# Pairing 64-row matmuls in the two halves of the TensorE array, with all eight PSUM banks in one rotation

## The chip, the cores and the metric

The kernel runs on one core of one Trainium2 chip. The metric is the device time of that core in microseconds (us), as the median of several executions. A profile comes from one of these executions; its span, from the first recorded instruction of the program to the end of the last, is about 1.7 us shorter than the timed value. For a kernel on one core, slow means over 1.5% above the fastest run of the same kernel. The medians are over all runs; where one of them was slow, the median of the fast ones stands beside it. Verdicts are given at 2%: "same" means that a difference of 2% isn't shown, not that there is none.

## The reference

Two branches over the same x are mixed with a gate. Branch A is a diagonal complex state-space scan over 2048 positions, branch B is a feed-forward network (FFN).

```python
x = A_x                                             # [1, 2048, 448]
g = sigmoid((x * gate_w).sum(-1, keepdims=True))
# A: Bu = x B_bar^T;  h_t = Lam_bar * h_(t-1) + Bu_t;  a = 2 Re(h C^T) + x * Dskip
# B: h = silu(x @ w1)          w1: [448, 1792]      "FFN1"
#    b = h @ w2                w2: [1792, 448]      "FFN2"
out = g * a + (1 - g) * b
```

FFN1 contracts over 448 rows. The array has 128 rows, so that is three full blocks and a remainder of 64 rows. This remainder is what the change is about.

## The kernel before

The program is written per engine. A small tracker gives every tile a name and makes an engine wait wherever it would read or overwrite a tile that another engine has not finished with. The eight PSUM banks are such tiles, `ps0` to `ps7`. Each engine runs its own list strictly in order.

FFN1 works in four chunks (even and odd positions, two halves each) of 14 blocks. The remainder is padded to 128 rows, with zeros in half of the rows of w1, so a block is four full matmuls:

```python
BK_F1 = [0, 1, 2, 3]                 # banks of FFN1
BK_F2 = BK_S = [4, 5, 6, 7]          # banks of FFN2, Bu, K0, Y
...
def ffn1(c, fb):
    bank = nxt(BK_F1, n_f1)
    ...
    def mm(pe):
        for j in range(4):           # 3 full blocks and one padded with 64 zero rows
            ins = pe.matmul(ps[:, bank, :], W[:, j, fb*128:(fb+1)*128],
                            XT[:, j0 + j, h*512:(h+1)*512], start=(j == 0), stop=(j == 3))
    T.op("pe", mm, reads=wk + xk, writes=[f"ps{bank}"])
    T.op("act", lambda e: e.activation(a[:, fb, :], ps[:, bank, :], AF.Silu), ...)
```

One small piece of branch A, the diagonal of Dskip, uses bank 7 by its number and not through a rotation:

```python
def side_diag():
    def mm(pe):                      # 4 matmuls with 2 rows (L464)
        ins = pe.matmul(ps[:, 7, pt*8:pt*8+2], RD[0:2, ...], ID[0:2, 0:2], ...)
    T.op("pe", mm, reads=["RD0", "RD1", "ID"], writes=["ps7"])
    T.op("dve", lambda e: e.tensor_copy(PV[:, :, 3:5], ps[:, 7, 0:32]...),   # L468
         reads=["ps7"], writes=["PVD"])
    ...                              # 8 small products, DE and DO
```

The order of the stages, which is each engine's order too:

```python
... ffn1(0, *) ; bu ; gate, scan(3) ; ffn1(1, *) ; scan(0) ; bu ; scan(1) ; scan(2)
ffn2(0, *) ; ffn1(2, *) ; ffn2(1, *)
run(coef)                            # side_diag, then CO and CE on VectorE
ffn1(3, *) ; ffn2(2, *) ; k0 ; ffn2(3, *) with ytile ...
```

VectorE comes to `side_diag`'s copy only when it has done all the scans.

Names in the profile lines: XT is x transposed; W1E and W1O hold w1 for even and odd positions, and until the gate is done the space of W1O holds a second copy of x (the line `W1O<-in_A_x_dram` is its load). Bu multiplies XT with LT, which holds the transposed B matrices; later the space of LT takes the results of FFN2. HS and Q belong to the scans on VectorE. CO and CE are tables that VectorE makes from C; K0 and Y are the last stages of branch A on TensorE, and K0 needs CO. A line such as `PE ps Lnnn <- DVE SG Lmmm: t, 1, t` says that TensorE's instruction at Lnnn waited for VectorE's at Lmmm, t us in all.

Of the kernel before, what the change touches and what calls it, by code (L numbers as in the profile page):

```python
# [8 lines left out]
AF = mybir.ActivationFunctionType  # L9

F32 = DT.float32
BF16 = DT.bfloat16
# [9 lines left out]
NFB = 14  # L22
NK = 1024
NKT = 8
# [120 lines left out]
def gated_mix(nc, A_x, A_Lambda_re, A_Lambda_im, A_B_re, A_B_im, A_C_re, A_C_im, A_log_dt,  # L145
              A_Dskip, B_x, B_w1, B_w2, gate_w, out):
    with ExitStack() as ctx:
        E = ctx.enter_context
        T = Tracker(nc, ctx)

        def sb(name, shape, dtype):
            return E(nc.sbuf_tensor(name, list(shape), dtype))
# [4 lines left out]
        XT = sb("XT", [128, 7, NK], BF16)  # L157
        W1E = sb("W1E", [128, 4, F_FF], BF16)
        W1O = sb("W1O", [128, 4, F_FF], BF16)
# [5 lines left out]
        CST = sb("CST", [112, 4, 256], BF16)  # L165
        CO = sb("CO", [128, 8, D], BF16)
        CE = sb("CE", [128, 8, D], BF16)
        KT = sb("KT", [128, 4, D], BF16)
        DE = sb("DE", [128, 4, 128], BF16)
        DO = sb("DO", [128, 4, 128], BF16)  # L170
# [3 lines left out]
        AT = [sb(f"AT{i}", [128, NFB, 512], BF16) for i in range(2)]  # L174
# [15 lines left out]
        Z = sb("Z", [128, 16], F32)  # L190
# [5 lines left out]
            return LTF[:, tile * D:(tile + 1) * D]  # L196

        ps = E(nc.psum_tensor("ps", [128, 8, 512], F32))
        BK_F1 = [0, 1, 2, 3]
        BK_F2 = BK_S = [4, 5, 6, 7]  # L200


        def ld(eng, dst, src, key, group=None):
            return T.dma(eng, lambda e: e.dma_start(dst, src), writes=[key], group=group)  # L204

        def ldt(dst, src, key, reads=(), group=None):
            return T.dma("sp", lambda e: e.dma_start_transpose(dst, src), reads=reads,
                         writes=[key], group=group)

        T.op("dve", lambda e: e.memset(Q1[:, 0, 0:512], 0.0), writes=["Q10"])  # L210
        T.op("dve", lambda e: e.memset(SG[0:64, 0:1], -1.0), writes=["SGa"])  # L211
# [10 lines left out]
        ld("act", W1E[0:64, 3, :], B_w1[384:448, :], "W1Ea")  # L222
        ld("act", W1E[:, 0:3, 0:512], B_w1[0:384, 0:512].rearrange("(j p) f -> p j f", p=128), "W1Eb")
        ld("act", W1E[:, 0:3, 512:], B_w1[0:384, 512:].rearrange("(j p) f -> p j f", p=128), "W1Ec")
        T.op("act", lambda e: e.activation(JK[:, 0, 0:1], HP[:, :], AF.Exp), reads=["HP"], writes=["JK0"])
        ldt(XT[:, 0:4, 0:512], x2[0:512, 0:512], "XTe0")
        ld("sp", BB[:, 0:6:2, D:], A_B_re[0:384, :].rearrange("(t p) d -> p t d", p=128), "Bre", gB)
        ld("sp", BB[:, 1:6:2, D:], A_B_im[0:384, :].rearrange("(t p) d -> p t d", p=128), "Bim", gB)
        ldt(XT[:, 4:7, 0:512], x2[0:512, 512:896], "XTo0")
        gB3 = T.group()  # L230
        for i, src in enumerate((A_B_re, A_B_im)):
            for h in range(2):
                ld("sp", Y3[h * 64:(h + 1) * 64, i, :], src[384:448, :], f"By{i}{h}", gB3)
        ldt(XT[:, 0:4, 512:1024], x2[512:1024, 0:512], "XTe1")
        ldt(XT[:, 4:7, 512:1024], x2[512:1024, 512:896], "XTo1")
        B_RAW = ["Bre", "Bim"]
        XC_ALL = ["XC0", "XC1"] + [f"XC3_{q}" for q in range(4)]
        B3 = ["By00", "By01", "By10", "By11"]
# [3 lines left out]
        T.op("pool", lambda e: e.affine_select(  # L242
            out=ID[:, :], in_=ID[:, :], pattern=[[-1, 128]], compare_op=ALU.is_equal, fill=0.0,
            base=0, channel_multiplier=1), reads=["ID"], writes=["ID"])
        T.op("pool", lambda e: e.memset(W1E[64:128, 3, :], 0.0), writes=["W1Ez"])
        T.op("pool", lambda e: e.iota(IOTA[:, :].bitcast(I32), pattern=[[1, NK]], base=0, channel_multiplier=0),
             writes=["IOTA"])
        T.op("pool", lambda e: e.tensor_copy(IOTA[:, :], IOTA[:, :].bitcast(I32)), reads=["IOTA"], writes=["IOTA"])
        T.op("pool", lambda e: e.memset(KT[64:128, 3, :], 0.0), writes=["KTz"])
        SGN = ["SGa", "SGb"]  # L250
# [3 lines left out]
             writes=["Rd"])  # L254
# [7 lines left out]
        def warm(n):  # L262
# [12 lines left out]
            reads=["ps6"], writes=["PV"])  # L275
# [12 lines left out]
        def c1(n, pt):  # L288
            i = pc(n)
            return P[:, i, pt:pt + 1]  # L290
# [32 lines left out]
        for o, up, low in (("ba", "lr", "li"), ("bb", "nli", "lr")):  # L323
# [10 lines left out]
            reads=["f2"] + SGN, writes=["f2s"])  # L334
# [47 lines left out]
        def step_B(pt):  # L382
            if pt < 3:
                lincombs([(BB[:, m, 0:D], f"BB{m}", BB[:, m, D:], c1("lr", pt), BB[:, m ^ 1, D:],
                           c1("li" if m % 2 else "nli", pt), B_RAW + ["lr", "li", "nli"])
                          for m in (2 * pt, 2 * pt + 1)])
# [62 lines left out]
        def side_C(odd):  # L449
            dst, key, b = (CO, "CO", "s") if odd else (CE, "CE", "e")  # L450
            for pt in range(3):
# [28 lines left out]
        XN = W1O[:, :, :].rearrange("p a b -> p (a b)")  # L480

        def load_xn():
            ld("sp", XN.rearrange("p (k c) -> p k c", k=NKT), x2.rearrange("(k p) c -> p k c", p=128), "XN")

        def gate():
            for t in range(2 * NKT):
                T.op("dve", lambda e, t=t: e.scalar_tensor_tensor(  # L487
                    JK[:, t % 2, :], XN[:, t * D:(t + 1) * D], 1.0, GWB[:, :],
                    ALU.mult, ALU.mult, accum_out=Z[:, t:t + 1]),
                    reads=["XN", "GW"], writes=[f"JK{t % 2}", f"Z{t}"])  # L490
                if t % 4 == 3:
                    yield
            yield
            zs = [f"Z{t}" for t in range(2 * NKT)]
            T.op("act", lambda e: e.activation(GT[:, 0, :], Z[:, :], AF.Tanh, scale=0.5),
                 reads=zs, writes=["GTt"])
            T.op("dve", lambda e: e.tensor_scalar(GT[:, 1, :], GT[:, 0, :], 0.5, 0.5, ALU.mult, ALU.add),
                 reads=["GTt"], writes=["GT1"])
            T.op("dve", lambda e: e.tensor_scalar(GT[:, 2, :], GT[:, 0, :], -0.5, 0.5, ALU.mult, ALU.add),
                 reads=["GTt"], writes=["GT2"])  # L500
            T.op("pool", lambda e: e.memset(W1O[0:64, 0, :], 0.0), writes=["XN", "W1Oz"])
            T.dma("sp", lambda e: e.dma_start(W1O[64:128, 0, :], B_w1[0:64, :]), reads=["W1Oz"],
                  writes=["W1Oa"])
            T.dma("sp", lambda e: e.dma_start(
                W1O[:, 1:4, :], B_w1[64:448, :].rearrange("(j p) f -> p j f", p=128)),
                reads=["W1Oz"], writes=["W1Ob"])
            yield


        n_f1 = [0]  # L510
        n_f2 = n_s = [0]

        def nxt(banks, n):
            b = banks[n[0] % len(banks)]
            n[0] += 1
            return b

        def ffn1(c, fb):
            odd, h = c // 2, c % 2
            bank = nxt(BK_F1, n_f1)  # L520
            W, j0 = (W1O, 3) if odd else (W1E, 0)
            a = AT[c % 2]
            wk = (["W1Oa", "W1Ob", "W1Oz"] if odd else
                  ["W1Ez", "W1Ea", "W1Eb"] if fb < 4 else ["W1Ez", "W1Ea", "W1Ec"])
            xk = [f"XTe{h}", f"XTo{h}"] if odd else [f"XTe{h}"]

            def mm(pe):
                ins = None
                for j in range(4):
                    ins = pe.matmul(ps[:, bank, :], W[:, j, fb * 128:(fb + 1) * 128],  # L530
                                    XT[:, j0 + j, h * 512:(h + 1) * 512],
                                    start=(j == 0), stop=(j == 3))
                return ins
            T.op("pe", mm, reads=wk + xk, writes=[f"ps{bank}"])
            T.op("act", lambda e: e.activation(a[:, fb, :], ps[:, bank, :], AF.Silu),  # L535
                 reads=[f"ps{bank}"], writes=[f"AT{c % 2}_{fb}"])

        def ffn2(c, q):
            odd, h = c // 2, c % 2
# [2 lines left out]
            a = AT[c % 2]  # L542
            bank = nxt(BK_F2, n_f2)

# [27 lines left out]
        def k0(j):  # L572
# [3 lines left out]
            def mm(pe):  # L576
                ins = None
                for m in range(7):
# [6 lines left out]
                 writes=[f"ps{bank}"])  # L585
            T.op("act", lambda e: e.activation(KT[0:M, j, :], ps[0:M, bank, 0:D], AF.Copy),
                 reads=[f"ps{bank}"], writes=[f"KT{j}"])

# [60 lines left out]
        def ytile(kt, odd):  # L649
            tile = 2 * kt + odd  # L650
            bank = nxt(BK_S, n_s)
            C, key = (CO, "CO") if odd else (CE, "CE")
            o0 = kt * 128 + (8 if odd else 7)
            t0 = kt * 128

            def mm(pe):
# [11 lines left out]
                else:  # L668
                    for j in range(4):
                        ins = pe.matmul(ps[:, bank, 0:D], XT[:, j, t0:t0 + 128], KT[:, j, :],  # L670
                                        start=False, stop=(j == 3))
                return ins
            xk = [f"XTe{kt // 4}", f"XTo{kt // 4}"]
            T.op("pe", mm, reads=hs_all + [f"{key}{m}" for m in range(7)] + xk
                 + [f"KT{j}" for j in range(4)] + ["KTz"] + [f"DO{j}" for j in range(4)],
                 writes=[f"ps{bank}"])
# [26 lines left out]
                    break  # L703

        tabs = chain(tables(0), tables(3))
        for fb in range(NFB):
            ffn1(0, fb)
            if fb in (8, 10, 12):
                run(tabs, 1)
        for h in range(2):  # L710
# [7 lines left out]
        s3 = scan(3)  # L718
        run(s3, 1)
        tabs = chain(tables(1), tables(2))  # L720
        for fb in range(NFB):
            ffn1(1, fb)
            if fb % 3 == 2:
                run(tabs, 1)
        run(gates)
# [16 lines left out]
        run(scan(2))  # L742
        for q in range(4):
            ffn2(0, q)
        for fb in range(NFB):
            ffn1(2, fb)
        for q in range(4):
            ffn2(1, q)
        run(coef)
        for fb in range(NFB):  # L750
            ffn1(3, fb)
        for q in range(4):
            ffn2(2, q)
        for j in range(4):
# [46 lines left out]
```

## Time and profile before

The median is 164.27 us over four runs (163.84 to 164.59); the first three gave 164.48 us.

| stage on TensorE, from the starts of its matmuls | starts at (us) | takes (us) |
|---|---|---|
| FFN1 chunk 0 (partly at half clock) | 10.20 | 14.68 |
| FFN1 chunk 1 | 33.95 | 12.09 |
| FFN1 chunk 2 | 68.72 | 12.09 |
| FFN2 chunk 1 | 80.80 | 10.69 |
| side diagonal | 91.49 | 0.18 |
| FFN1 chunk 3 | 91.67 | 12.10 |
| FFN2 chunks 2 and 3, K0, Y and the last store | 103.77 | 59.0 |

The next lines are from the first two parts of the page of the kernel before. The first line gives busy time by engine. The rows below it show 40 equal slices of the span (4.07 us each): busy tenths, and in the PEclk row the clock that TensorE was granted.

```profile
PE 154.5 (95%) x774; PEld 74.4 (46%) x774; DVE 109.8 (67%) x216; ACT 67.8 (42%) x111; POOL 7.3 (4%) x16
...
PE   6549999999999999999999999999999999999992
...
DVE  0559999306999999999999999999401131133342
...
PEclk9955999999999999999999999999999999999999
```

TensorE has hardly a gap after the start. VectorE's 67% hides a second, nearly full stretch: from slice 10 to slice 27 (the first is slice 0) it is 90% busy or more. So there is a second long chain close behind the first.

The chain of waits of the kernel before, in order of time (start, length, what), shows which of the two counts. These are pieces from its middle:

```profile
68.88 12.09 PE ps L530 x56
80.97 10.59 PE ps L548 x56
91.56 0.18 PE ps L464 x4
91.74 12.19 PE ps L530 x56
103.93 10.59 PE ps L548 x56
```

TensorE runs into itself, stage after stage. The head of the same view on the page, shares of the span by engine, says it in one line:

```profile
PE 92%; DMA 4%; ACTq 1%; DVE 0%; issue 0%
```

The waits of TensorE in the kernel before (for whom, us in total, times, longest) are all in the first 10.2 us:

```profile
PE ps L530 <- DMA W1E<-in_B_w_dram: 3.3, 1, 3.3
PE ps L266 <- DVE SG L211: 1.3, 1, 1.3
PE ps L259 <- issue: 0.6, 1, 0.6
```

Two lines of VectorE's timeline before (start, length, instruction, and in brackets the idle time ahead of it) give the ends of its stretch up to the diagonal's copy:

```profile
38.09 0.63 DVE L487 SCALAR_TENSOR_TENSOR JK<-W1O,GWB 128x448 bf16<-128x448 bf16 x1 [8.17 <-DMA W1O<-in_A_x_dram]
...
100.62 0.16 DVE L468 COPY PV<-ps 128x8 f32<-128x8 f32 x1
```

VectorE starts when x has landed a second time, at 38.07 us, and reads bank 7 at 100.62 us. TensorE wrote that bank at 91.5 us. The result lies in bank 7 for nine microseconds, and nobody else wants the bank: FFN1 has banks 0 to 3.

### The profile page before, as it was taken

Reading aid. Unit: us, or ns where it says so; the run is one execution under the profiler, and the core shown is the slowest. Engines: PE = TensorE matmul, PEld = TensorE weight load, DVE = VectorE, ACT = ScalarE, POOL = GpSimd, SP = SyncE. Lnnn points to the kernel's source line nnn. Section 1 sums busy time; section 2 is a strip of 40 time slices with the busy share of each in tenths; the row PEclk is TensorE's granted clock in tenths of the full one; section 3 lists DMA queues with packets and bytes.
Section 4 is the critical chain, followed back from the end, with each engine's and each line's share of the span. In section 5 each row is a group of like instructions: output and inputs, shape, how many; then the busy total and the mean of one; then the engine's idle time right before and its main releaser. Section 6 shows DMA issues by size and latency. Waiting matters only on the chain.

```text
span 162.8 us, 2017 instructions
## 1 busy us (share of the span) xinstructions
PE 154.5 (95%) x774; PEld 74.4 (46%) x774; DVE 109.8 (67%) x216; ACT 67.8 (42%) x111; POOL 7.3 (4%) x16
## 2 busy tenths in 40 slices
PE   6549999999999999999999999999999999999992
PEld 2113444444444455544455444455555555555551
DVE  0559999306999999999999999999401131133342
ACT  0614699759976522267622376431421101100000
POOL 7500000000030000000000000000000000000000
PEclk9955999999999999999999999999999999999999
DMA  4999999899207884000000000000000101101211
GB/s 101 265 354 214 211 174 141 165 365 352 69 0 229 260 154 89 14 0 0 4 0 0 0 0 0 6 0 0 0 0 0 60 0 56 56 0 71 101 57 56
DMA packets 26387, 14.76 MB, mean 91 GB/s; under 512 B 19845, under 2 KB 25226, under 8 KB 26378
## 3 DMA queue, kind: packets, MB, share of 16 engines
q1 hardware_dynamic: 25492, 13.03, 31.6%
q10 hardware_dynamic: 886, 1.61, 3.2%
q8 instruction: 6, 0.10, 0.3%
q14 instruction: 3, 0.02, 0.0%
HBM read 7.92 MB, written 1.84 MB: 60 GB/s over the span
## 4 chain that ended last, share of the span: by engine, by line
PE 92%; DMA 4%; ACTq 1%; DVE 0%; issue 0%
PE ps L530 31%; PE ps L548 26%; PE ps L659 13%; PE ps L564 13%; DMA W1E<-in_B_w_dram 4%; PE ps L670 4%; PE ps L579 3%; ACTq L204 1%; PE ps L666 1%; DVE OT L678 0%; PE ps L662 0%; PE ps L581 0%; PE ps L464 0%
## 5 line engine op out<-in xcount | busy, mean ns | idle before, releaser
L548 PE MATMUL ps<-W,AT 128*128 128x448 bf16 x224 | 43.5, 353 | 0.0
L535 ACT ACTIVATE AT<-ps 128x512 bf16<-128x512 f32 x56 | 32.7, 597 | 15.8 <-PE ps L530 15.7
L678 DVE SCALAR_TENSOR_TENSOR OT<-ps,GT,LT 128x448 bf16<-128x448 f32 x16 | 10.9, 684 | 33.6 <-PE ps L670 26.9
L548 PEld LDWEIGHTS ps<-W,AT 128*128 128x128 bf16 x224 | 21.7, 98 | 20.1 <-issue 0.2
L530 PE MATMUL ps<-XT,W1E 128*128 128x512 bf16 x112 | 27.1, 407 | 3.3 <-DMA W1E<-in_B_w_dram 3.3
L553 ACT ACTIVATE LT<-ps,GT 128x448 bf16<-128x448 f32 x16 | 10.1, 633 | 43.4 <-PE ps L548 43.4
L530 PE MATMUL ps<-XT,W1O 128*128 128x512 bf16 x112 | 24.5, 379 | 0.0
L564 PE MATMUL ps<-XT,LT 128*128 128x512 bf16 x98 | 21.5, 379 | 0.0
L530 PEld LDWEIGHTS ps<-XT,W1E 128*128 128x128 bf16 x112 | 11.5, 103 | 18.8 <-issue 7.3
L530 PEld LDWEIGHTS ps<-XT,W1O 128*128 128x128 bf16 x112 | 10.9, 98 | 12.9
L600 DVE TENSOR_TENSOR_SCAN G<-P,Q 128x1024 f32<-128x1024 f32 x7 | 15.7, 2277 | 0.0
L564 PEld LDWEIGHTS ps<-XT,LT 128*128 128x128 bf16 x98 | 9.6, 98 | 11.6
L487 DVE SCALAR_TENSOR_TENSOR JK<-W1O,GWB 128x448 bf16<-128x448 bf16 x16 | 8.8, 622 | 8.2 <-DMA W1O<-in_A_x_dram 8.2
L659 PE MATMUL ps<-CO,HS 128*128 128x448 bf16 x56 | 11.9, 352 | 0.0
L659 PE MATMUL ps<-CE,HS 128*128 128x448 bf16 x56 | 11.9, 352 | 0.0
L568 ACT ACTIVATE HS<-ps 128x512 bf16<-128x512 f32 x14 | 8.4, 598 | 6.8 <-PE ps L564 6.6
L597 DVE TENSOR_TENSOR Q<-G,SIN 128x1024 bf16<-128x1024 f32 x7 | 8.5, 1218 | 0.0
L597 DVE TENSOR_TENSOR Q<-G,COS 128x1024 bf16<-128x1024 f32 x7 | 8.5, 1209 | 0.0
L659 PEld LDWEIGHTS ps<-CO,HS 128*128 128x128 bf16 x56 | 5.5, 98 | 5.1
L670 PE MATMUL ps<-KT,XT 128*128 128x448 bf16 x32 | 7.4, 352 | 0.0
L659 PEld LDWEIGHTS ps<-CE,HS 128*128 128x128 bf16 x56 | 5.3, 98 | 4.4
L266 PE MATMUL ps<-Q 128*128 128x512 bf16 x12 | 4.8, 569 | 1.3 <-DVE SG L211 1.3
(75 smaller groups left out, 114.9 us busy)
## 6 DMA issues: line engine op xcount, KB each, us to landing
W1O<-in_A_x_dram SPq DMA_DIRECT2D x1, 1792.0 KB, 9.8
out_dram<-OT SPq DMA_DIRECT2D x8, 224.0 KB, 1.9
W<-in_B_w_dram SPq DMA_DIRECT2D x1, 1568.0 KB, 14.0
W1O<-in_B_w_dram SPq DMA_DIRECT2D x1, 1344.0 KB, 7.4
W1E<-in_B_w_dram ACTq DMA_DIRECT2D x1, 960.0 KB, 9.7
W1E<-in_B_w_dram ACTq DMA_DIRECT2D x1, 384.0 KB, 7.3
BB<-in_A_B_re_dram SPq DMA_DIRECT2D x1, 336.0 KB, 6.8
BB<-in_A_B_im_dram SPq DMA_DIRECT2D x1, 336.0 KB, 8.6
```

The source lines that it names most:

```text
L487: T.op("dve", lambda e, t=t: e.scalar_tensor_tensor(JK[:, t % 2, :], XN[:, t * D:(t + 1) * D], 1.0, GWB[:, :], ALU.mult, ALU.mult, accum_o ...
L530: ins = pe.matmul(ps[:, bank, :], W[:, j, fb * 128:(fb + 1) * 128], XT[:, j0 + j, h * 512:(h + 1) * 512], start=(j == 0), stop=(j == 3))
L535: T.op("act", lambda e: e.activation(a[:, fb, :], ps[:, bank, :], AF.Silu), reads=[f"ps{bank}"], writes=[f"AT{c % 2}_{fb}"])
L548: ins = pe.matmul(ps[:, bank, 0:D], a[:, fb, q * 128:(q + 1) * 128], W2[:, fb, :], start=(fb == 0), stop=(fb == NFB - 1))
L553: T.op("act", lambda e: e.activation(bs(tile), ps[:, bank, 0:D], AF.Copy, scale=GT[:, 2, tile:tile + 1]), reads=[f"ps{bank}", "GT2"], writ ...
L564: ins = pe.matmul(ps[:, bank, :], LT[:, m, j, :], XT[:, j, h * 512:(h + 1) * 512], start=(j == 0), stop=(j == 6))
L568: T.op("act", lambda e: e.activation(HS[:, m, 8 + h * 512:8 + (h + 1) * 512], ps[:, bank, :], AF.Copy), reads=[f"ps{bank}", f"F{pt}"], wri ...
L597: T.op("dve", lambda e: e.tensor_tensor(o, a, b, op), reads=reads, writes=writes)
L600: T.op("dve", lambda e: e.tensor_tensor_scan(G[:, c, :], rb, Q1[:, c, :], 0.0, ALU.mult, ALU.add), reads=[f"Q1{c}", "rr"], writes=[f"G{c}"])
L659: ins = pe.matmul(ps[:, bank, 0:D], HS[:, m, o0:o0 + 128], C[:, m, :], start=(m == 0), stop=False)
L670: ins = pe.matmul(ps[:, bank, 0:D], XT[:, j, t0:t0 + 128], KT[:, j, :], start=False, stop=(j == 3))
L678: T.op("dve", lambda e: e.scalar_tensor_tensor(o[:, odd * D:(odd + 1) * D], ps[:, bank, 0:D], GT[:, 1, tile:tile + 1], bs(tile), ALU.mult, ...
```

## The change

The intent is to stop spending a full matmul on 64 rows. The two remainders of a pair of blocks are run at the same time, one in the lower and one in the upper 64 rows of the array. For that, the 64 rows of w1 are loaded into both halves, and a copy `XR` of the matching rows of x is made with its halves swapped (four copies from SBUF to SBUF). Four blocks form a batch: 12 full matmuls, then two pairs. A batch holds four banks at once, so all stages now share one rotation of eight.

```diff
-        BK_F1 = [0, 1, 2, 3]
-        BK_F2 = BK_S = [4, 5, 6, 7]
+        BK_F1 = BK_F2 = BK_S = list(range(8))
...
+        def xr_early(h):                       # on the sync queue
+            T.dma("sp", lambda e: e.dma_start(XR[64:128, hs], XT[0:64, 3, hs]), reads=[f"XTe{h}"], ...)
+            T.dma("sp", lambda e: e.dma_start(XR[0:64, hs], XT[64:128, 3, hs]), reads=[f"XTe{h}"], ...)
...
+        ld("act", W1E[64:128, 3, :], B_w1[384:448, :], "W1Ez")   # was a memset to zero
...
         ldt(XT[:, 4:7, 0:512], ..., "XTo0")
+        xr_early(0)
         ... Y loads; ldt XTe1; ldt XTo1
+        xr_early(1)
...
-        n_f1 = [0]
-        n_f2 = n_s = [0]
+        n_f1 = n_f2 = n_s = [0]
...
+            for fb, bank in zip(fbs, banks):
+                def mm(pe, ...):               # three full matmuls of each block
...
+            def rest(pe):
+                for i, (fb, bank) in enumerate(zip(fbs, banks)):
+                    up = (i % 2 == 1 and not single) != bool(odd)
+                    p = slice(64, 128) if up else slice(0, 64)
+                    x = XT[p, 3, hs] if up == bool(odd) else XR[p, hs]
+                    ins = pe.matmul(ps[:, bank, :], W[p, jr, ...], x, start=False, stop=True)
...
+            for f0 in range(0, NFB, 4):
+                yield from ffn1(c, list(range(f0, min(f0 + 4, NFB))), single and f0 == 0)
```

`side_diag` is not touched. (The very first batch is unpaired, `single`, so that it need not wait for the copies. The loads of W1O lose a memset that they used to wait for.)

More of the change, by code (lines that the diff above doesn't have):

```diff
@@ L167, in gated_mix @@
         CE = sb("CE", [128, 8, D], BF16)
+        XR = sb("XR", [128, NK], BF16)
         KT = sb("KT", [128, 4, D], BF16)
@@ L208, in ldt @@
                          writes=[key], group=group)
+        def xr_early(h):
+            hs = slice(h * 512, (h + 1) * 512)
+            T.dma("sp", lambda e: e.dma_start(XR[64:128, hs], XT[0:64, 3, hs]), reads=[f"XTe{h}"],
+                  writes=[f"XR{h}a"])
+            T.dma("sp", lambda e: e.dma_start(XR[0:64, hs], XT[64:128, 3, hs]), reads=[f"XTe{h}"],
+                  writes=[f"XR{h}b"])
         T.op("dve", lambda e: e.memset(Q1[:, 0, 0:512], 0.0), writes=["Q10"])
@@ L244, in gated_mix @@
             base=0, channel_multiplier=1), reads=["ID"], writes=["ID"])
-        T.op("pool", lambda e: e.memset(W1E[64:128, 3, :], 0.0), writes=["W1Ez"])
         T.op("pool", lambda e: e.iota(IOTA[:, :].bitcast(I32), pattern=[[1, NK]], base=0, channel_multiplier=0),
@@ L483, in load_xn @@
             ld("sp", XN.rearrange("p (k c) -> p k c", k=NKT), x2.rearrange("(k p) c -> p k c", p=128), "XN")
+        XN_DONE = [f"Z{2 * NKT - 1}"]
         def gate():
@@ L500, in gate @@
                  reads=["GTt"], writes=["GT2"])
-            T.op("pool", lambda e: e.memset(W1O[0:64, 0, :], 0.0), writes=["XN", "W1Oz"])
-            T.dma("sp", lambda e: e.dma_start(W1O[64:128, 0, :], B_w1[0:64, :]), reads=["W1Oz"],
+            T.dma("sp", lambda e: e.dma_start(W1O[0:64, 0, :], B_w1[0:64, :]), reads=XN_DONE,
+                  writes=["W1Oz"])
+            T.dma("sp", lambda e: e.dma_start(W1O[64:128, 0, :], B_w1[0:64, :]), reads=XN_DONE,
                   writes=["W1Oa"])
@@ L505, in gate @@
                 W1O[:, 1:4, :], B_w1[64:448, :].rearrange("(j p) f -> p j f", p=128)),
-                reads=["W1Oz"], writes=["W1Ob"])
+                reads=XN_DONE, writes=["W1Ob"])
             yield
-        n_f1 = [0]
-        n_f2 = n_s = [0]
+        n_f1 = n_f2 = n_s = [0]
         def nxt(banks, n):
@@ L516, in nxt, with ffn1 @@
             return b
-        def ffn1(c, fb):
+        def ffn1(c, fbs, single=False):
             odd, h = c // 2, c % 2
-            bank = nxt(BK_F1, n_f1)
-            W, j0 = (W1O, 3) if odd else (W1E, 0)
+            hs = slice(h * 512, (h + 1) * 512)
+            W, w0, x0, jr = (W1O, 1, 4, 0) if odd else (W1E, 0, 0, 3)
             a = AT[c % 2]
             wk = (["W1Oa", "W1Ob", "W1Oz"] if odd else
-                  ["W1Ez", "W1Ea", "W1Eb"] if fb < 4 else ["W1Ez", "W1Ea", "W1Ec"])
+                  ["W1Ez", "W1Ea", "W1Eb"] if fbs[-1] < 4 else ["W1Ez", "W1Ea", "W1Ec"])
@@ L525, in ffn1 @@
             xk = [f"XTe{h}", f"XTo{h}"] if odd else [f"XTe{h}"]
-            def mm(pe):
-                ins = None
-                for j in range(4):
-                    ins = pe.matmul(ps[:, bank, :], W[:, j, fb * 128:(fb + 1) * 128],
-                                    XT[:, j0 + j, h * 512:(h + 1) * 512],
-                                    start=(j == 0), stop=(j == 3))
-                return ins
-            T.op("pe", mm, reads=wk + xk, writes=[f"ps{bank}"])
-            T.op("act", lambda e: e.activation(a[:, fb, :], ps[:, bank, :], AF.Silu),
-                 reads=[f"ps{bank}"], writes=[f"AT{c % 2}_{fb}"])
+            banks = [nxt(BK_F1, n_f1) for _ in fbs]
@@ new lines, in ffn1, with mm @@
+            for fb, bank in zip(fbs, banks):
+                def mm(pe, fb=fb, bank=bank):
+                    ins = None
+                    for j in range(3):
+                        ins = pe.matmul(ps[:, bank, :], W[:, w0 + j, fb * 128:(fb + 1) * 128],
+                                        XT[:, x0 + j, hs], start=(j == 0), stop=False)
+                    return ins
+                T.op("pe", mm, reads=[k for k in wk if k != "W1Ez"] + xk, writes=[f"ps{bank}"])
+            def rest(pe):
+                ins = None
+                for i, (fb, bank) in enumerate(zip(fbs, banks)):
+                    up = (i % 2 == 1 and not single) != bool(odd)
+                    p = slice(64, 128) if up else slice(0, 64)
+                    x = XT[p, 3, hs] if up == bool(odd) else XR[p, hs]
+                    ins = pe.matmul(ps[:, bank, :], W[p, jr, fb * 128:(fb + 1) * 128], x,
+                                    start=False, stop=True)
+                return ins
@@ new lines, in ffn1, with ffn1_chunk @@
+            T.op("pe", rest, reads=[k for k in wk if k != "W1Ez" or not single] + xk + ([] if single else [f"XR{h}a", f"XR{h}b"]),
+                 writes=[f"ps{bank}" for bank in banks])
+            for fb, bank in zip(fbs, banks):
+                T.op("act", lambda e, fb=fb, bank=bank: e.activation(a[:, fb, :], ps[:, bank, :], AF.Silu),
+                     reads=[f"ps{bank}"], writes=[f"AT{c % 2}_{fb}"])
+                yield
+        def ffn1_chunk(c, single=False):
+            for f0 in range(0, NFB, 4):
+                yield from ffn1(c, list(range(f0, min(f0 + 4, NFB))), single and f0 == 0)
@@ L705, in gated_mix @@
         tabs = chain(tables(0), tables(3))
-        for fb in range(NFB):
-            ffn1(0, fb)
+        for fb, _ in enumerate(ffn1_chunk(0, single=True)):
             if fb in (8, 10, 12):
@@ L720, in gated_mix @@
         tabs = chain(tables(1), tables(2))
-        for fb in range(NFB):
-            ffn1(1, fb)
+        for fb, _ in enumerate(ffn1_chunk(1)):
             if fb % 3 == 2:
@@ L744, in gated_mix @@
             ffn2(0, q)
-        for fb in range(NFB):
-            ffn1(2, fb)
+        for fb, _ in enumerate(ffn1_chunk(2)):
+            pass
         for q in range(4):
@@ L749, in gated_mix @@
         run(coef)
-        for fb in range(NFB):
-            ffn1(3, fb)
+        for fb, _ in enumerate(ffn1_chunk(3)):
+            pass
         for q in range(4):
```

## The prediction

> **What bounds it now.** The chain of waits gives TensorE 92% of the 162.8 us span: from 10.2 us to 159.7 us the matmuls run back to back. In the timeline, full 512-column matmuls start 0.216 us apart. FFN1 is 224 of them (four chunks of 14 blocks x 4), 12.09 us a chunk when warm.
> Close behind runs VectorE: it starts the gate products when the second copy of x lands (38.07 us) and is then busy almost without a gap until 115.9 us. The copy of the diagonal out of PSUM bank 7 (L468) starts at 100.62 us, 8.9 us after TensorE wrote it (L464, 91.6 us). Nobody minds before, because FFN1 uses banks 0-3 only.
>
> **Intended gain.** 26 pairs of 64-row matmuls in place of 52 full ones: 26 x 0.216 = 5.6 us if the pairs overlap. The Trainium skill, "TensorEngine Tiling (Array Packing)", Key Properties, says that changing the tiling mode drains TensorE. The trace agrees: around the two-row matmuls of L464 about 0.10 us going in and 0.07 us coming out are lost. 16 batches x 0.17 = 2.7 us back, so about 2.9 us net on TensorE.
>
> **What it costs.**
> 1. The side diagonal still writes bank 7, and FFN1 now rotates through all eight. Chunk 3's eighth block falls on bank 7; the built program shows a VectorE wait there. So TensorE stops after 16 + 9 matmuls of chunk 3 until VectorE has finished the last scan and L468. Earlier gains only lengthen this stop.
> 2. VectorE gets later. The sync queue now waits for the transposes of x (XT of the second half landed at 18.40 us) and issues four copies (about 0.6 us each, as the Y loads took) before the seven LT transposes, which started at 17.16 us. I expect them some 3.8 us later and the load of x (issued 28.23 us, 9.8 us to landing) about 2.5 us later. VectorE then reaches L468 at about 103.1 us.
> 3. TensorE reaches block 7 of chunk 3 at about 96 us and idles some 7 us. "TensorE: Matmul & The Clock Gate", Part 1, gives a window of about 3.4 us after which an idle array falls to half clock. This trace agrees: its clock was 0.5 from 8.7 to 15.5 us after the early gap. I expect half clock again for 3.4 to 6.8 us, about 2.5 us lost.
>
> **Sum.** Stop ends at 103.4 us. Left of chunk 3: 21 full matmuls + 5 pairs = 26 x 0.216 = 5.6 us, six mode changes 0.5 us, cold clock 2.5 us: FFN1 ends at about 112 us, against 103.93 us. From there TensorE bounds as before. +8.1 us: **172.5 us**, range 169.8 to 175.0. Chances: faster by over 2% 0.03, within 2% 0.05, slower by over 2% 0.92.
>
> **What would show it.** A TensorE wait of 5 to 9 us in chunk 3, released by VectorE's L468; a second half-clock stretch in the clock row just after; L468 at 101 to 105 us; the x load landing 1 to 4 us later; chunk 2 of FFN1 shorter than 12.09 us by about 0.8 us, pairs starting a few ns apart; everything from the third FFN2 chunk on unchanged in length.
>
> **What would make it wrong.** If the x load is not delayed, 170 us. If the pairs don't overlap, only about 1 us more shows. If the wait on bank 7 were not there: about 162 us.

## The result, and the profile after

The changed kernel takes 173.24 us (172.80 to 173.35, four runs) against 164.27 us. The ratio is 1.0543, with a 95% interval of 1.0509 to 1.0576. Here and below, a ratio is the mean time of one kernel's fast runs over that of the other's fast runs of the same rounds, so it is not quite the ratio of the medians quoted. The output is correct.

| stage on TensorE | before: starts, takes | after: starts, takes |
|---|---|---|
| FFN1 chunk 0 | 10.20, 14.68 | 9.77, 13.83 |
| FFN1 chunk 1 | 33.95, 12.09 | 32.68, 11.42 |
| FFN1 chunk 2 | 68.72, 12.09 | 66.78, 11.41 |
| FFN2 chunk 1 | 80.80, 10.69 | 78.20, 11.58 |
| side diagonal | 91.49, 0.18 | 89.78, 0.17 |
| FFN1 chunk 3 | 91.67, 12.10 | 89.95, 22.54 |
| everything later | 103.77, 59.0 | 112.49, 59.0 |

The whole loss is in one line. TensorE comes to chunk 3 of FFN1 1.7 us earlier than before and leaves it 8.7 us later; the rest is equal. The sum over chunk 3: 8.26 us of stop and about 2.7 us of half clock (both shown below), less the 0.7 us that the pairs save, make about the 10.4 us by which it is longer. The corresponding lines of the page of the changed kernel (40 slices of 4.29 us) show the place:

```profile
PE 154.9 (90%) x774; PEld 69.8 (41%) x774; DVE 108.8 (63%) x216; ACT 63.5 (37%) x111; POOL 4.1 (2%) x14
...
PE   7679999999999999999989208999999999999992
...
DVE  0567999103999999999999999996000311323332
...
PEclk9969999999999999999999955799999999999999
```

TensorE is nearly idle in slices 22 and 23 (94 to 103 us), and its clock drops in slices 23 to 25. VectorE is full in both of these slices. The chain of waits of the changed kernel, by engine, now runs through VectorE for 43% of the span, where it had none of it before:

```profile
DVE 43%; PE 38%; DMA 8%; SPq 8%; issue 1%
```

The waits of TensorE in the changed kernel name what ended the idle time:

```profile
PE ps L543 <- DVE PV L477: 8.3, 1, 8.3
...
PE ps L473 <- ACT LT L583: 0.8, 1, 0.8
```

L477 is the copy out of bank 7, L468 of before. The second line is a smaller thing of the same kind: FFN2's rotation ended on bank 7 just before the diagonal (L473), which therefore waits 0.8 us for ScalarE to empty it. The timeline of both engines around the stop:

```profile
93.18 2.12 PE L543 MATMUL ps<-XT,W1O 128*128 128x512 bf16 x9
...
103.34 0.16 DVE L477 COPY PV<-ps 128x8 f32<-128x8 f32 x1
...
103.55 1.46 PE L543 MATMUL ps<-XT,W1O 128*128 128x512 bf16 x3 [8.26 <-DVE PV L477]
...
105.92 4.38 PE L543 MATMUL ps<-XT,W1O 128*128 128x512 bf16 x12
...
110.76 1.47 PE L543 MATMUL ps<-XT,W1O 128*128 128x512 bf16 x6
```

Nine matmuls are blocks 4, 5 and 6 of chunk 3; the next three, of block 7, go to bank 7 and wait 8.26 us. The 12 full matmuls at 105.92 us take 4.38 us where 12 full ones elsewhere take 2.76 us. The clock records of the trace put half clock from 99.0 to 109.2 us.

The pairs themselves do what they were made for. These lines are from chunk 2, with the matmul form as rows*columns of the array:

```profile
69.47 0.39 PE L554 MATMUL ps<-XT,W1O 64*128 64x512 bf16 x1
69.47 0.39 PE L554 MATMUL ps<-XR,W1O 64*128 64x512 bf16 x1
69.69 0.38 PE L554 MATMUL ps<-XT,W1O 64*128 64x512 bf16 x1
69.70 0.38 PE L554 MATMUL ps<-XR,W1O 64*128 64x512 bf16 x1
70.01 2.76 PE L543 MATMUL ps<-XT,W1O 128*128 128x512 bf16 x12
```

The two of a pair start together (3 ns apart in the raw records), and the next pair follows after 0.22 us. Between the last pair and the full matmuls lie 0.31 us, 0.09 us more than the usual spacing of 0.216 us: this is the mode change.

The sync queue's timeline explains why VectorE is later. It begins the gate products when the x load has landed; in the changed kernel this is:

```profile
41.52 0.63 DVE L498 SCALAR_TENSOR_TENSOR JK<-W1O,GWB 128x448 bf16<-128x448 bf16 x1 [10.80 <-DMA W1O<-in_A_x_dram]
```

The sync queue, first before, then after:

```profile
12.66 4.39 SPq L207 DMA_TRANSPOSE XT<-in_A_x_dram  x2
17.16 10.39 SPq L207 DMA_TRANSPOSE LT<-BB  x7
...
28.23 0.43 SPq L204 DMA_DIRECT2D W1O<-in_A_x_dram  x1
```

```profile
14.15 3.80 SPq L207 DMA_TRANSPOSE XT<-in_A_x_dram  x2
19.31 0.48 SPq L212 DMA_DIRECT2D XR<-XT  x1
19.83 0.60 SPq L214 DMA_DIRECT2D XR<-XT  x1
20.55 9.77 SPq L207 DMA_TRANSPOSE LT<-BB  x7
...
30.99 0.43 SPq L204 DMA_DIRECT2D W1O<-in_A_x_dram  x1
```

The queue waits 1.3 us for x's transposes before it can issue the last two copies, and everything behind them moves: the LT transposes by 3.4 us, the x load by 2.8 us. The x load lands 3.4 us later (41.49 us), and VectorE copies bank 7 2.7 us later.

### The profile page after: what moved, and what is told of

It reads as the page before. It is cut to its first block, busy times and chain, and to the rows that moved or that the text cites. A ratio compares the mean times of both kernels' runs of the same rounds, so it can differ in the third digit from the quotient of the medians.

```text
span 171.5 us, 2024 instructions
## 1 busy us (share of the span) xinstructions
PE 154.9 (90%) x774; PEld 69.8 (41%) x774; DVE 108.8 (63%) x216; ACT 63.5 (37%) x111; POOL 4.1 (2%) x14
## 4 chain that ended last, share of the span: by engine, by line
DVE 43%; PE 38%; DMA 8%; SPq 8%; issue 1%
DVE Q L627 17%; PE ps L578 12%; PE ps L689 12%; DVE G L630 9%; DMA W1O<-in_A_x_dram 6%; SPq L207 5%; DVE JK L498 5%; PE ps L543 4%; PE ps L700 4%; PE ps L609 3%; DVE HS L627 3%; SPq L204 2%; DMA Y<-in_A_B_im_dram 2%; DVE BB L387 2%; DVE HS L357 1%; DVE G L355 1%
## 5 line engine op out<-in xcount | busy, mean ns | idle before, releaser
L560 ACT ACTIVATE AT<-ps 128x512 bf16<-128x512 f32 x56 | 29.5, 605 | 34.3 <-PE ps L554 34.3
L543 PE MATMUL ps<-XT,W1O 128*128 128x512 bf16 x84 | 21.9, 412 | 8.3 <-DVE PV L477 8.3
L583 ACT ACTIVATE LT<-ps,GT 128x448 bf16<-128x448 f32 x16 | 10.1, 633 | 42.1 <-PE ps L578 40.1
L543 PE MATMUL ps<-XT,W1E 128*128 128x512 bf16 x84 | 21.2, 404 | 2.9 <-issue 2.9
L543 PEld LDWEIGHTS ps<-XT,W1O 128*128 128x128 bf16 x84 | 8.0, 103 | 21.1 <-DVE PV L477 8.8
L543 PEld LDWEIGHTS ps<-XT,W1E 128*128 128x128 bf16 x84 | 8.1, 103 | 15.9 <-issue 7.7
L598 ACT ACTIVATE HS<-ps 128x512 bf16<-128x512 f32 x14 | 7.9, 615 | 0.3 <-POOL HS L370 0.3
L275 PE MATMUL ps<-Q 128*128 128x512 bf16 x12 | 5.5, 627 | 1.3 <-DVE SG L218 1.3
## 6 DMA issues: line engine op xcount, KB each, us to landing
W1E<-in_B_w_dram ACTq DMA_DIRECT2D x1, 960.0 KB, 10.1
```

The lines of the kernel that those rows point to most:

```text
L543: ins = pe.matmul(ps[:, bank, :], W[:, w0 + j, fb * 128:(fb + 1) * 128], XT[:, x0 + j, hs], start=(j == 0), stop=False)
L560: T.op("act", lambda e, fb=fb, bank=bank: e.activation(a[:, fb, :], ps[:, bank, :], AF.Silu), reads=[f"ps{bank}"], writes=[f"AT{c % 2}_{fb}"])
L583: T.op("act", lambda e: e.activation(bs(tile), ps[:, bank, 0:D], AF.Copy, scale=GT[:, 2, tile:tile + 1]), reads=[f"ps{bank}", "GT2"], writ ...
```

## The experiments

The theory has three parts. (A) The eight-bank rotation makes FFN1 need bank 7, which the diagonal holds until VectorE is through with its scans. (B) The copies in the sync queue make VectorE later and the stop longer. (C) The stop lets the clock fall, which costs more. The main rivals are that the pairing with its mode changes costs more than it saves, and that the extra DMA traffic, rather than its place in the queue, is the delay. All runs below gave correct output. Each has one profile. How far one profile can be trusted shows in two of the same program: the copy of bank 7 began at 103.34 us in the changed kernel and at 104.18 us when the same kernel was run again. Runs of one group ran on the same chip, beside the same runs of the kernel before.

### First group: the parts alone (before: 163.45 us)

**rot8_alone.** The kernel before with the rotation and nothing else:

```diff
-        BK_F1 = [0, 1, 2, 3]
-        BK_F2 = BK_S = [4, 5, 6, 7]
+        BK_F1 = BK_F2 = BK_S = list(range(8))
...
-        n_f1 = [0]
-        n_f2 = n_s = [0]
+        n_f1 = n_f2 = n_s = [0]
```

> The kernel before with nothing but the single rotation of eight banks. If the stop on bank 7 is the cause, FFN1 chunk 3 must stop here too: TensorE should reach its eighth block at about 98.5 us (91.7, plus 0.7 us for an eviction of bank 7 ahead of the side diagonal, plus seven blocks of 0.864) and wait for VectorE's copy of the diagonal until 100.8 us: about 3 us in all, 167.3 us, no new half-clock stretch [...]. If the rotation is harmless and the pairing or the copies are the cause, 164.3 us.

Measured: 168.47 us (168.24 us without the one slow run of four), ratio 1.0258 (1.0171 to 1.0345; with three fast runs the interval is wide and the verdict at 2% is unclear). Of TensorE's waits in this run, two belong to bank 7:

```profile
PE ps L528 <- DVE PV L467: 3.4, 1, 3.4
...
PE ps L463 <- ACT LT L551: 0.8, 1, 0.8
```

Both waits are there without a pair, a copy or a mode change. Chunk 3 takes about 15.66 us against 12.10 (its first matmul is missing from the records; from the diagonal's first matmul to the next FFN2 chunk it is 15.84 us against 12.28). This settles (A). The stop is 1.1 us longer than expected, since in this run TensorE got there earlier and VectorE later than I had put down; there is no second half-clock stretch in the profiled run (the slow run, 171.70 us, has no profile). The stop is shorter than in the changed kernel because TensorE comes later and VectorE earlier. A faster TensorE only waits longer here.

**seven_banks.** The changed kernel, with bank 7 left to the diagonal:

```diff
-        BK_F1 = BK_F2 = BK_S = list(range(8))
+        BK_F1 = BK_F2 = BK_S = list(range(7))
```

> The changed kernel with bank 7 left out of the rotation (seven banks). If the stop on bank 7 is the whole loss: no long TensorE wait in chunk 3, no half-clock stretch, and the net gain of the pairing (about 2.4 us by the batch periods of the changed kernel's trace) shows: 162 us, between 161 and 163. If the pairing with its mode changes or the later VectorE chain are themselves the loss, it stays above 164.3 us.

Measured: 162.13 us, ratio 0.9898 (0.9846 to 0.9950). One line of code takes back the loss and leaves a gain of 1%, small but clear of the noise. The stop is gone, and there is no half clock in the middle. What is left of the lateness shows in two new, small waits of TensorE in this kernel:

```profile
PE ps L594 <- DMA LT<-BB: 0.6, 1, 0.6
PE ps L609 <- issue: 0.4, 1, 0.4
```

The first is the first Bu stage waiting for a late LT transpose. The second stands ahead of the K0 stage (L609), which needs CO: VectorE finished CO at 112.3 us, and K0 began at 112.4 us, with the FFN2 chunk ahead of it 0.58 us longer than elsewhere. The view says "issue" for it; that it is CO I infer from these times. So the second chain is right behind the first again.

**seven_unpaired.** The same with all remainders in the same half, so that none can overlap; batches, copies and mode changes stay:

```diff
-                    up = (i % 2 == 1 and not single) != bool(odd)
+                    up = bool(odd)
```

> As seven_banks, but all 64-row matmuls go to the same half of the array, so none can overlap; batches, mode changes and copies stay. If the pairs overlap fully, this is 26 x 0.216 = 5.6 us slower than seven_banks: about 167.6 us. If the pairing gains nothing, the same as seven_banks.

Measured: 167.40 us, ratio 1.0204 (1.0133 to 1.0275; unclear at 2%), 5.3 us above seven_banks. The four remainders of a batch now follow each other, four in 1.03 us:

```profile
73.06 1.03 PE L554 MATMUL ps<-XT,W1O 64*128 64x512 bf16 x4
```

A clean figure comes from the traces, away from the start where the clock wavers. From the first matmul of FFN2 chunk 0 to that of FFN2 chunk 1, which spans one whole FFN1 chunk, it is 22.68 us before, 22.01 us in the changed kernel and 23.51 us here. The pairs save 1.50 us a chunk, seven times 0.216 us, so they overlap fully. Against the kernel before, the eight mode changes of a chunk cost 0.83 us, or 0.10 us each. The rival that pairing is a loss falls; it is a net gain of 0.67 us a chunk, though more than half of the gross gain goes to the mode changes.

**copies_on_act.** The changed kernel, with the four copies issued by ScalarE's queue:

```diff
-            T.dma("sp", lambda e: e.dma_start(XR[64:128, hs], XT[0:64, 3, hs]), ...)   # and the other
+            T.dma("act", lambda e: e.dma_start(XR[64:128, hs], XT[0:64, 3, hs]), ...)
...
         pact("cs", col("afr"), AF.Sin, ...)
+        xr_early(0)
...
         for fb, _ in enumerate(ffn1_chunk(0, single=True)):
+            if fb == 6:
+                xr_early(1)
```

> The changed kernel with the four copies issued by ScalarE's queue, which has nothing to do at those moments, in place of the sync queue. If the sync queue's wait and issue time make VectorE late, the x load lands at 38 to 39 us again, L477 starts at about 101 us, and the time falls by about 2.2 us to 171 us. If it is the extra DMA traffic that makes it late, it stays at 173.2 us.

Measured: 171.11 us, ratio 1.0447 (1.0381 to 1.0512): the expected time, but not by the expected way. The x load landed at 39.4 us, 2.1 us earlier than in the changed kernel and still 1.3 us later than before, so the place in the queue is most of the delay. The remaining 1.3 us are there already when the LT transposes are issued (18.41 us against 17.16 before), since the queue spent longer on the transposes of x ahead of them. Whether the extra DMA traffic does that was not tested. But L476, the copy of bank 7, began at 102.52 us, only 0.8 us earlier. The remaining 1.2 us of the gain came from the clock: half clock from 99.1 to 105.9 us, so that chunk 3 took 7.7 us after the stop and not 8.9 us. Part of this may be chance: the changed kernel run again (after_again, below) took 8.3 us there. One line of VectorE's timeline in this run shows where the rest of the earlier x load went:

```profile
59.27 0.69 DVE L626 TENSOR_TENSOR HS<-Q 128x1024 bf16<-128x1024 bf16 x1 [1.19 <-DMA Q<-Q]
```

### Second group: what was left open (before: 163.98 us)

**swap_first.** VectorE waited there for the two half swaps `Q<-Q` of a scan. The W1O loads stand ahead of these swaps in the same queue, as they did before; the change makes them three in place of two and lets them start 0.03 us after VectorE's last gate product in place of 1.7 us. Here the loads go behind the swaps:

```diff
-            T.dma("sp", ... W1O ...)      # three loads, at the end of gate()
+            yield
+        def load_w1o(): ...               # the same three loads
...
         run(s3, 1)
+        load_w1o()
```

> The kernel copies_on_act with the three W1O loads issued after the two half swaps of the third scan in place of before them. In copies_on_act the x load landed 2.1 us earlier than in the changed kernel but L476 started only 0.8 us earlier, and VectorE waited 1.2 us for the swap's landing. If the swap was held up behind the W1O loads, the wait goes and L476 starts at about 101.3 us: about 1.2 us less than copies_on_act, 169.9 us. If not, L476 stays at 102.5 us and the time at 171.1 us.

Measured: 170.91 us, ratio 1.0429 (1.0382 to 1.0477). The wait is gone (the second swap landed 2.3 us after its issue, in place of 4.8 us), and L476 began at 101.54 us, 1.0 us earlier, as expected. This is one profile each; the same wait was 0 us in the changed kernel and 0.75 us in after_again, so the size is uncertain. The time did not follow: chunk 3 took 8.4 us after the stop against 7.7 us in copies_on_act, since half clock lasted until 106.3 us. What the earlier end of the stop gives, the moment at which the clock recovers takes back in part. This is a miss in time and a hit in mechanism.

**stop_filled.** The changed kernel, with 34 useless matmuls into bank 0 (which is empty by then) ahead of the stopped block. The stop stays; only TensorE is busy in it:

```diff
             for fb, bank in zip(fbs, banks):
+                if c == 3 and fb == 7:
+                    def fill(pe):
+                        for _ in range(34):
+                            ins = pe.matmul(ps[:, 0, :], W[:, 1, 0:128], XT[:, 4, hs], start=True, stop=True)
+                    T.op("pe", fill, ..., writes=["ps0"])
```

> The changed kernel with 34 useless matmuls (7.3 us warm) put into bank 0 just ahead of the stopped block, so that TensorE works while it would idle; the wait on bank 7 and its end at 103.5 us stay. If the half clock after the stop is a loss of its own, chunk 3 ends at about 109.8 us in place of 112.5, the clock row has no second dip, and the time is about 170.4 us. If the clock after the stop costs nothing, 173.2 us.

Measured: 171.83 us (171.38 us without the one slow run of four), ratio 1.0470 (1.0407 to 1.0533), less of a gain than expected. In the profiled run the clock stayed full and chunk 3 took 6.25 us after the stop against 8.94 us, but L477 began at 105.06 us, 1.7 us later than in the changed kernel. The filling cannot have caused that: VectorE's scan that began at 64.55 us in the changed kernel began at 66.27 us here, 1.7 us late already, some thirty microseconds before the first useless matmul. The pair was run again on one chip all the same (third group).

**diag_early.** A repair that keeps eight banks: the copies on ScalarE's queue as in copies_on_act, and the whole diagonal moved to where VectorE idles for the x load:

```diff
+        ld("act", RD[0:1, 0:D], row(A_Dskip), "RD0", gRD)      # and RD1, behind the W1E loads
...
-        coef = chain(side_coef(), side_diag(), side_C(True), side_C(False))
+        coef = chain(side_coef(), side_C(True), side_C(False))
...
         load_w2()
+        run(side_diag())
         run(gates, 5)
```

> The repaired change: copies on ScalarE's queue, and the side diagonal (its two loads, four matmuls, copy and eight products) moved to about 34 us, where VectorE idles for the x load; eight banks and batches of four stay. No stop on bank 7, and VectorE about 1.6 us ahead of copies_on_act, so CO is ready before TensorE asks. TensorE bound throughout: 0.68 us saved in each of three chunks and some 0.4 us in the first: about 2.4 us under before.

Measured: 162.02 us, ratio 0.9901 (0.9858 to 0.9944). The copy of bank 7 runs at 33.4 us, CO is finished at 108.9 us, and K0 starts without a wait at 111.4 us. TensorE bounds again, and the gain is about 2 us in medians (1.6 us by the ratio), a little less than the expected 2.4 us.

**six_six_two.** The same with larger batches:

```diff
-            for f0 in range(0, NFB, 4):
-                yield from ffn1(c, list(range(f0, min(f0 + 4, NFB))), single and f0 == 0)
+            for f0, f1 in ((0, 4), (4, 10), (10, 14)) if c == 0 else ((0, 6), (6, 12), (12, 14)):
+                yield from ffn1(c, list(range(f0, f1)), single and f0 == 0)
```

> As diag_early with batches of 6, 6 and 2 blocks (4, 6, 4 in the first chunk), so six mode changes in a chunk in place of eight. At the 0.10 us a change that the unpaired run gives (0.83 us a chunk over eight), about 0.2 us less in each chunk: 0.8 us under diag_early, unless ScalarE, which now gets six blocks at once, makes TensorE wait for banks.

Measured: 161.67 us, ratio 0.9874 (0.9836 to 0.9911). From FFN2 chunk 0 to FFN2 chunk 1 it is 21.80 us against 22.00 us in diag_early: the 0.2 us a chunk are there. In total only 0.35 us show, because TensorE waited 1.0 us for an LT transpose at the first Bu stage. The intervals of the two kernels overlap.

### Third group: the clock again, and a better kernel (before: 164.04 us)

**after_again** is the changed kernel unaltered, and **stop_filled_again** is stop_filled unaltered, on one chip.

> The changed kernel unaltered, to stand beside stop_filled on one chip, since the runs so far were on different chips or at different times: 173 us, the stop ending at 103 to 104 us, half clock after it.

> stop_filled unaltered. In its first run chunk 3 took 6.25 us after the stop against 8.94 us in the changed kernel, but its stop ended 1.7 us later, so the time fell by less than expected. If the half clock costs 2.7 us of its own, then on the same chip this is 2 to 3 us under after_again, with the stop ending at the same time in both. If the filling itself delays VectorE, the stop ends later again and the difference is about 1 us.

Measured: 173.58 us (173.43 us without the one slow run of six), ratio 1.0549 (1.0499 to 1.0599), and 171.10 us, ratio 1.0439 (1.0399 to 1.0478). The intervals don't overlap, and the means of the fast runs differ by 1.9 us. The wait for L477, first in after_again, then in stop_filled_again, where the filling has taken its place:

```profile
PE ps L543 <- DVE PV L477: 8.7, 1, 8.7
```

```profile
PE ps L552 <- DVE PV L477: 0.8, 1, 0.8
```

The copy of bank 7 began at 104.18 us and at 103.70 us, so the filling does not delay VectorE; the 1.7 us of the first run were variation of that run. After the stop, chunk 3 took 8.30 us and 6.25 us. The PEclk rows, first of after_again, then of stop_filled_again:

```profile
PEclk9969999999999999999999955899999999999999
```

```profile
PEclk9858999999999999999999999999999999999999
```

The dip in the middle is gone although the stop is not. The half clock is a loss of its own, 2.05 us in this pair of profiles and 2.69 us against the first profile of the changed kernel. This is (C).

**late_pairs.** Chunk 0 keeps its four full matmuls with zero rows, so no extra load, copy or wait stands at the start of the kernel. The second copy of the weight rows and the copies of x are issued after chunk 0; chunks 1 to 3 are paired in batches of 6, 6 and 2; the diagonal is early.

```diff
+        def ffn1_whole(c):                # ffn1 of the kernel before, on the eight-bank rotation
+            ...
+            ld("act", W1E[64:128, 3, :], B_w1[384:448, :], "W1Ez")
+            xr_early(1, "act")
...
         load_w2()
+        xr_early(0, "sp")
+        run(side_diag())
```

> Pairs only in chunks 1 to 3 (batches 6, 6, 2), chunk 0 as before with its zero rows; the second copy of the weight rows and the copies of x are issued after chunk 0, so the start of the kernel carries no extra DMA and no extra wait; side diagonal early. Saves 0.89 us in each of three chunks (12.09 - 11.20): 2.7 us under before, about 0.4 us under six_six_two, whose TensorE waited 1.0 us for an LT transpose at the first Bu stage.

Measured: 161.56 us, ratio 0.9840 (0.9813 to 0.9868), 2.5 us under before in medians.

**late_pairs_warm.** One more edit, outside the change, but suggested by (C). In every profile so far the start of FFN1 ran at half clock after 2.9 to 4.0 us without matmuls:

```diff
-        warm(3)
+        warm(17)
```

> As late_pairs with 17 in place of 3 idle matmuls after the column matmuls, which fill the idle time ahead of FFN1. Every kernel so far had half clock for 3.4 or 6.8 us at the start of FFN1. If idleness ahead of it is the cause, the clock stays full, chunk 0 takes 12.1 in place of 14 to 14.7 us, and the time falls by another 1.7 to 2.6 us, unless VectorE (CO at about 109 us) then holds up the K0 stage, which I expect to take back up to 1 us.

Measured: 159.38 us, ratio 0.9723 (0.9685 to 0.9760): faster than both kernels by more than 2%. Chunk 0 takes 12.09 us in place of 14.76, and the clock row is full from where its records begin, at 10.1 us (the digits of the first two slices, 4 us each, are no reading):

```profile
PEclk9999999999999999999999999999999999999999
```

K0 did not wait. In the profiled run, the slowest of its six, the 17 matmuls ran until 11.7 us, which delayed FFN1 by nearly 2 us against late_pairs. They started 0.43 us apart up to 9.9 us and 0.216 us apart from 10.2 us on: in this profile the half clock was spent on the useless matmuls and not on FFN1. A smaller number may do better. I did not try one.

## Why the prediction was right, point by point

- **The stop.** Predicted: TensorE stops after 16 + 9 matmuls of chunk 3 until L468, for 5 to 9 us, ending at 103.4 us. Measured: 8.26 us, ending at 103.55 us. rot8_alone shows that the rotation alone makes it, and seven_banks that it goes with bank 7. I also wrote about 162 us for the case without the wait; seven_banks gave 162.1 us.
- **VectorE's delay.** Predicted: the x load 2.5 us later and L468 at 103.1 us. Measured: 3.4 us later, and 103.34 us. In the first profile some of the delay was absorbed on the way. copies_on_act shows that the place in the sync queue is most of it (2.1 of 3.4 us).
- **The clock.** Predicted: about 2.5 us lost to half clock. Measured by filling the stop: 2.05 to 2.69 us in the profiles; the timed runs of the pair on one chip differ by 1.9 us in the mean.
- **The gain.** Predicted: mode changes of 0.17 us for a batch, chunk 2 shorter by about 0.8 us. Measured: 0.19 us for a batch (0.10 going in, 0.09 coming out) and 0.68 us. The pairs overlap fully. With the stop in place, almost none of this reaches the end, since TensorE's early arrival is waited away.
- **What was missing.** The prediction's text did not name the 0.8 us that the diagonal itself waits for ScalarE to empty bank 7. It falls ahead of the stop, so it only shortens the stop. In rot8_alone it is 0.8 us of the same detour.
- **The sum.** 112 us for the end of FFN1 against 112.49 us measured; 172.5 us against 173.24 us. What remains is mostly the clock term (about 0.2 us), the stop's end (0.15 us) and mode changes slightly dearer than assumed.
- **A side remark that was off.** The text says that without the delay of the x load the time is 170 us. swap_first comes near that case, with L476 at 101.54 us, and takes 170.9 us, because half clock lasted until 106.3 us. The remark counted the clock as a constant; it varies from profile to profile.

The pages of the Trainium skill carried two steps. "TensorEngine Tiling (Array Packing)", Key Properties, says that a change of tiling mode drains TensorE: the trace shows a loss of 0.10 us at each change, which fits. "TensorE: Matmul & The Clock Gate", Part 1, says that an idle array falls to half clock in windows of about 3.4 us: the traces agree in part. Their half-clock stretches lasted 3.4, 6.8 and 10.2 us, but the clock did not wait for 3.4 us of idleness to fall. The prediction called the early stretch agreement; there the fall came 1.8 us after the last matmul ended (8.67 against 6.86 us). The forecast of a second half-clock stretch assumed a stop of some 7 us, well beyond 4.0 us, the longest that a fall took in these profiles.

## What to carry to other kernels

When buffers that were split between stages are merged into one rotation, look for everything that uses one of them by a fixed number, and ask when its last reader runs in that engine's own order; a value that lay there for nine microseconds without harm becomes a stop. Before counting a gain on the busiest engine, look for the chain just behind it: here it set the end of the stop, and every microsecond gained ahead of it was waited away. A stop of TensorE can cost more than its length: here a stop of 8 us brought 2 to 2.7 us of half clock with it, and one of 3.4 us (rot8_alone, in its profile) none. So price the clock after it as well.

## What the Trainium skill lacked or had wrong

- "TensorEngine Tiling (Array Packing)", Key Properties, says that a mode change drains TensorE but gives no size. The runs show 0.10 us a change (0.83 us for the eight changes of a chunk), which is nearly half of a 512-column matmul (0.216 us) and eats 55% of what the pairs save.
- "TensorE: Matmul & The Clock Gate", Part 3, lists the speedups of packing with 3, 4, 9 and 16 tiles but not of two row tiles. Two tiles of 64 rows, with 512 columns streamed through each, gave the full factor of two: 1.50 us saved in a chunk, which is seven times 0.216 us, before the mode changes. Its start distance of about 4 ns within a pack agrees (3 ns here).
- The same page, Part 1, has the clock recover about 4 us into sustained matmuls, within 500 ns. Here, after the stop, it took 3.2, 4.4, 4.6 and 5.7 us in copies_on_act, after_again, swap_first and the changed kernel. It also says that the clock falls after an idle window of about 3.4 us. In the stop it fell 2.9 us (after_again) to 4.0 us (copies_on_act) after the last matmul ended, while a stop of 3.4 us in rot8_alone passed without a drop in the profiled run. Ahead of FFN1 it fell as early as 0.8 us (rot8_alone) and 1.3 us (swap_first) after the last matmul, and the 3.4 us before these two falls held 1.6 and 1.7 us of matmul time, so the window need not be idle throughout.
- "TensorEngine Tiling (Array Packing)", Gotcha 1, warns of PSUM pressure from tiling, but only of tiles that share a bank. The costly case here was a bank held by an unrelated small result (8.3 us). No page read has it.
